# Reordering the first batch of a fused attention and feed-forward kernel: scores further ahead, casts and copies on other engines, loads in another order

## The chip, the cores and the metric

The kernel runs on one core of a Trainium2 chip. The metric is the device time of one execution in microseconds; lower is better. Executions of one kernel differ by 1 to 6 us here, so every comparison is made against executions of the kernel before on the same chip in the same rounds.

## The reference

Eight batches of eight heads of causal attention (576 positions, 64 wide, with a bias from a cumulative sum of `s`), then a gated feed-forward on all 4608 tokens:

```python
scores = q @ k.T / 8 ;  cum = cumsum(max(s, 0))
scores = where(causal, -1e9, scores + min(-(cum[i] - cum[j]), 0))
x = (softmax(scores) @ v)            # [B, H, 576, 64] -> [4608, 512]
g = x @ w_gate                       # 512 x 1536
out = (g * sigmoid(g) * (x @ w_val)) @ w_out
```

Inputs and output are float32; the kernel computes in bfloat16 with float32 sums.

## The kernel before

Heads are taken in half-batches of four. A half-batch's q and k are loaded ("raw"), cast to bfloat16 (ck, cq), transposed on TensorE and copied from PSUM into one of two KQ buffers; 64 more rows of KQ hold the bias, split into parts (HL), brought by small DMAs (`aug`). For each head TensorE makes scores, ScalarE takes the exponential, GpSimd masks the diagonal, TensorE multiplies with V (AV), VectorE normalises (ot), and TensorE transposes into x. The first batch of eight heads runs alone. After that the feed-forward of one tile of 512 tokens and the attention of the next batch are interleaved in one fixed TensorE order.

```python
# one queue (Sync) issues nearly all loads, in program order
def load_one(hb, name, rs=(0, NR)): ... nc.sync.dma_start(loaded[name, hb] ...)   # 2304-byte pieces
def load_v(b, cs):
    ...                                # one raw V buffer; rows of 64 floats: 256-byte pieces
    nc.sync.dma_start(t[0:n, c, :, :], v[b, :, c*128 : c*128+n, :].rearrange("h p d -> p h d"))
...
def prep_one(hb, i):                   # a quarter of a half-batch's q and k into KQ
    pe_transpose(hb, nm, g)
    pe_out(hb, nm, g, 0, nc.vector)
    pe_out(hb, nm, g, 1, nc.scalar)
...
def first_batch():
    avq = {4: (0,), 5: (1, 2), 6: (3, 4), 7: (5, 6, 7)}     # AV pieces behind head h's scores
    wq = {0: ("g", 0), 1: ("v", 0), 3: ("g", 1), 5: ("v", 1)}   # weight loads, GpSimd's queue
    for h in range(H):
        for ci in range(4):
            score_piece(h, ci)
        ...
    init_vt(1)
    aug(3, SP4)                        # Sync queue from here:
    load_v(1, range(5))                # V of batch 1
    load_qk(3)                         # k and q of half-batch 3
    load_qk(4)
    x_pe(H // 2 - 1)
...
hook = {                               # while the first feed-forward tile runs
    1: [cast_one(2, "k"), cast_one(2, "q")],
    2: [prep_one(2, 0)], 3: [prep_one(2, 1)], 4: [prep_one(2, 2)], 5: [prep_one(2, 3)],
    8: [cast_one(3, "k", nc.gpsimd), cast_one(3, "q", nc.gpsimd)],
    21: [load_qk(5)],
}
```

(Cuts are marked; the hook's lambdas are abbreviated.)

The softmax here doesn't subtract the row's maximum and nothing guards it: scores larger than these inputs give would overflow.

## Time and profile before

| | before |
|---|---|
| time, median of the first three runs | 409.08 us (407.78 to 409.84) |
| span of the profiled execution | 406.5 us |
| TensorE busy | 384.8 us, 95% |
| first feed-forward matmul | 34.40 us |
| first scores of the second batch | 46.51 us, after a wait of 2.52 us |

The prediction below shows the slices, the windows and the waits that it rests on. A line is start, length, engine, source line, operation, tiles and count; in brackets the idle time before it and what ended that.

```profile
44.90 1.15 POOL L230 CAST ck<-rawk 128x1152 bf16<-128x1152 f32 x1 [11.20 <-DMA rawk<-in_k_dram]
```
```profile
48.40 0.72 PE L272 MATMUL bank<-ident,ck 128*128 128x128 bf16 x5
```

GpSimd waited 11.20 us for k of half-batch 3 and cast it as soon as it landed, at 44.90. TensorE took up the result at 48.40, without a wait. So the transfer had 2.35 us to spare (48.40 - 44.90 - 1.15), in a kernel that the change wanted to bring forward by 5 us.

### The profile page before, as it was taken

The page shows a single profiled execution, that of the slowest core. Times are in us where ns is not written, and L with a number is a line of the kernel's source. Part 1 is how long each engine was busy: PE and PEld are TensorE (multiplying, and loading weights), DVE is VectorE, ACT ScalarE, POOL GpSimd, SP SyncE. Part 2 cuts the span into 40 slices and gives each one's busy share as a digit, 9 for nine tenths or more (in the row PEclk, how much of TensorE's full clock was granted, in tenths as well). Part 3 has the DMA queues.
Part 4 walks back from the last instruction along what each step waited for, and adds up shares of the span by engine and source line. Part 5 has one row for each costly group of instructions (what it writes and reads, how often), then busy time and mean ns, then how long its engine had stood idle before and what let it go on. Part 6 is the DMA issues. An engine that isn't in the chain of part 4 may idle for free.

```text
span 406.5 us, 8052 instructions
## 1 busy us (share of the span) xinstructions
PE 384.8 (95%) x3100; PEld 213.0 (52%) x3100; DVE 249.1 (61%) x487; ACT 212.0 (52%) x407; POOL 125.0 (31%) x225
## 2 busy tenths in 40 slices
PE   2778799999999999999999999999999999999996
PEld 2664355655555555555555555555555554444442
DVE  7755658547863696368835784489447733852760
ACT  6742566855555655555545654655555542322321
POOL 6852444732442235222613162316211110000000
PEclk9988899999999999999999999999999999999999
DMA  7999899398635784579356944681510002002002
GB/s 242 188 250 212 267 192 269 133 272 190 178 93 194 174 206 118 173 194 211 102 157 192 247 72 127 214 167 51 120 57 0 2 27 78 0 16 89 2 1 103
DMA packets 85288, 56.71 MB, mean 140 GB/s; under 512 B 65489, under 2 KB 69553, under 8 KB 85249
## 3 DMA queue, kind: packets, MB, share of 16 engines
q1 hardware_dynamic: 81440, 51.44, 47.0%
q0 software_dynamic: 3808, 4.76, 6.9%
q8 instruction: 24, 0.39, 0.4%
q14 instruction: 16, 0.12, 0.1%
HBM read 37.90 MB, written 15.93 MB: 132 GB/s over the span
## 4 chain that ended last, share of the span: by engine, by line
PE 89%; DVE 4%; ACT 2%; DMA 2%; POOL 1%; issue 1%; ACTq 0%; SPq 0%
PE bank L546 23%; PE bank L518 22%; PE bank L533 22%; PE bank L347 9%; PE bank L385 7%; PE bank L420 3%; PE wide L347 1%; DMA kq<-HL 1%; PE one L385 1%; DMA s_sb<-in_s_dram 1%; ACT th L523 1%; POOL vt L171 1%; DVE pp L525 1%; DVE kq L301 1%; ACT pt L360 1%
## 5 line engine op out<-in xcount | busy, mean ns | idle before, releaser
L360 ACT ACTIVATE pt<-bank 128x512 bf16<-128x512 f32 x224 | 104.2, 505 | 42.4 <-PE bank L347 35.1
L525 DVE SCALAR_TENSOR_TENSOR pp<-th,bank 128x512 bf16<-128x512 bf16 x108 | 74.2, 687 | 65.2 <-ACT th L523 64.6
L518 PE MATMUL bank<-xt,wg 128*128 128x512 bf16 x432 | 112.1, 382 | 0.7 <-DVE xt L425 0.7
L533 PE MATMUL bank<-xt,wv 128*128 128x512 bf16 x432 | 112.5, 383 | 0.0
L523 ACT ACTIVATE th<-bank 128x512 bf16<-128x512 f32 x108 | 64.5, 597 | 81.6 <-PE bank L518 79.8
L546 PE MATMUL bank<-wo,ht 128*128 128x512 bf16 x432 | 105.7, 379 | 0.0
L363 POOL TENSOR_SCALAR_AFFINE_SELECT pt<-pt 128x512 bf16<-128x512 bf16 x64 | 40.8, 638 | 127.1 <-ACT pt L360 124.7
L538 DVE TENSOR_TENSOR ht<-pp,bank 128x512 bf16<-128x512 bf16 x108 | 73.8, 684 | 7.4
L347 PE MATMUL bank<-kq 128*128 128x128 bf16 (+4 forms) x504 | 66.7, 241 | 3.3 <-DVE kq L301 2.5
L347 PEld LDWEIGHTS <-kq 128*128 128x128 bf16 x576 | 46.1, 100 | 40.2 <-issue 4.2
L518 PEld LDWEIGHTS <-wg 128*128 128x128 bf16 x432 | 38.6, 98 | 36.9 <-issue 1.9
L533 PEld LDWEIGHTS <-wv 128*128 128x128 bf16 x432 | 38.9, 99 | 35.2 <-issue 1.7
L546 PEld LDWEIGHTS <-ht 128*128 128x128 bf16 x432 | 38.1, 98 | 34.9
L385 PEld LDWEIGHTS <-pt 128*128 128x128 bf16 x960 | 41.1, 98 | 19.0 <-issue 1.9
L385 PE MATMUL bank<-vt,pt 128*128 128x65 bf16 x840 | 44.0, 194 | 0.0
L554 ACT ACTIVATE ysb<-bank 128x512 f32<-128x512 f32 x36 | 21.5, 597 | 42.9 <-PE bank L546 41.4
L368 POOL TENSOR_SCALAR_AFFINE_SELECT pt<-pt 128x64 bf16<-128x64 bf16 x64 | 15.3, 239 | 63.4 <-ACT pt L360 60.7
L402 DVE TENSOR_TENSOR ot<-bank,rc 128x320 bf16<-128x320 f32 x56 | 27.5, 492 | 1.9
L424 DVE COPY xt<-bank 128x128 bf16<-128x128 bf16 (+6 forms) x28 | 9.0, 321 | 31.7 <-PE bank L420 31.0
L401 DVE RECIPROCAL rc<-bank 128x5 f32<-128x5 f32 x56 | 10.6, 190 | 25.2 <-PE bank L385 25.2
L171 POOL CAST vt<-rawv 128x512 bf16<-128x512 f32 (+1 forms) x40 | 25.8, 673 | 0.0
L230 POOL CAST ck<-rawk 128x1152 bf16<-128x1152 f32 x15 | 17.4, 1159 | 11.5 <-DMA rawk<-in_k_dram 11.5
(59 smaller groups left out, 191.6 us busy)
## 6 DMA issues: line engine op xcount, KB each, us to landing
out_dram<-ysb SPq DMA_DIRECT2D x36, 256.0 KB
rawk<-in_k_dram SPq DMA_DIRECT2D x15, 576.0 KB
rawq<-in_q_dram SPq DMA_DIRECT2D x15, 576.0 KB
rawv<-in_v_dram SPq DMA_DIRECT2D x32, 256.0 KB
ks<-ck SPq DMA_DIRECT2D x11, 288.0 KB
qs<-cq SPq DMA_DIRECT2D x11, 288.0 KB
wg<-in_moe_w_gate_dram POOLq DMA_DIRECT2D x2, 768.0 KB, 12.0
wv<-in_moe_w_val_dram POOLq DMA_DIRECT2D x2, 768.0 KB, 13.6
```

The costliest lines, as they stand in the source:

```text
L171: eng.tensor_copy(VT[b % 2][0:n, c, :, 0:D], loaded["v", b][0:n, c, :, :])
L347: nc.tensor.matmul(sc[:, o : o + w], T[:, 1, e * S + 128 * tj : e * S + 128 * (tj + 1)], T[:, 0, e * S + lo : e * S + hi], start=True, sto ...
L360: nc.scalar.activation(pt[:, c0 : c0 + W], sc[:, 0:W], AF.Exp, scale=0.125)
L363: nc.gpsimd.affine_select(pt[:, 1088:1600], pt[:, 1088:1600], pattern=[[0, 4], [1, 128]], compare_op=ALU.is_ge, fill=zreg, base=0, channel ...
L385: nc.tensor.matmul(av[:, bi * (D + 1) : (bi + 1) * (D + 1)], pt[:, c0 : c0 + 128], VT[b % 2][:, tj, h, :], start=(tj == 0), stop=(tj == bi),)
L402: nc.vector.tensor_mul(ot[:, :, e * D : (e + 1) * D], av3[:, :, 0:D], rc[:, :, None].to_broadcast([128, NCH, D]),)
L518: nc.tensor.matmul(pg, WG[j][:, c, f0 : f0 + 128], xt[:, c, :], start=(c == 0), stop=(c == 3),)
L523: nc.scalar.activation(th, pg, AF.Tanh, scale=0.5)
L525: nc.vector.scalar_tensor_tensor(pp, in0=th, scalar=1.0, in1=pg, op0=ALU.add, op1=ALU.mult)
L533: nc.tensor.matmul(pv, WV[j][:, c, f0 : f0 + 128], xt[:, c, :], start=(c == 0), stop=(c == 3),)
L538: nc.vector.tensor_mul(ht, pp, pv)
L546: nc.tensor.matmul(py, hts[ft][:, ts_ * 128 : (ts_ + 1) * 128], WO[ft // WKO][:, ft % WKO, :], start=(ft == 0), stop=(ft == NFT - 1),)
```

## The change

Its intent: let the scores of the first batch run a head further ahead of AV, so that ScalarE's exponentials don't wait; split the V casts between GpSimd and VectorE; and copy half of half-batch 2's KQ on ScalarE before the feed-forward. To make the first scores earlier, q of half-batch 1 is loaded later. Two loads move with the code around them: V of batch 1 is now issued behind head 5, in front of the HL copies of half-batch 3, and the gate's second weight half moves by a head. The core of the diff (the zeroing of the bias rows and the size of a buffer of ones also change):

```diff
-        load_qk(1)
+        load_one(1, "k")
...
         cast_half(0, "k", 0, nc.scalar)
-        cast_half(0, "q", 0, nc.gpsimd)
+        cast_half(0, "q", 0, nc.scalar)
         aug(0, SP4)
+        load_one(1, "q")
         load_v(0, range(5))
         load_qk(2)
-        aug(1, [nc.gpsimd] * 4)
...
-        cast_one(1, "k", nc.gpsimd)
+        cast_one(1, "k", nc.vector)
...
-            avq = {4: (0,), 5: (1, 2), 6: (3, 4), 7: (5, 6, 7)}
-            wq = {0: ("g", 0), 1: ("v", 0), 3: ("g", 1), 5: ("v", 1)}
+            avq = {5: (0,), 6: (1, 2), 7: (3, 4, 5, 6)}
+            wq = {0: ("g", 0), 1: ("v", 0), 4: ("g", 1), 5: ("v", 1)}
...
+                    for c in range(3, 5):
+                        cast_v(0, c, nc.vector)
...
                 if h == 3:
-                    for c in range(3, 5):
-                        cast_v(0, c, nc.gpsimd)
                     aug(2, SP4)
+                    init_vt(1)
+                if h == 5:
+                    cast_one(2, "k", nc.gpsimd)
+                    load_v(1, range(5))
+                if h == 6:
+                    cast_one(2, "q", nc.gpsimd)
+                if h == 7:
+                    aug(3, SP4)
+                    load_qk(3)
+                    load_qk(4)
...
-            init_vt(1)
-            aug(3, SP4)
-            load_v(1, range(5))
-            load_qk(3)
-            load_qk(4)
+            for nm in ("k", "q"):
+                pe_transpose(2, nm, 0)
+                for r in range(2):
+                    pe_out(2, nm, 0, r, nc.scalar)
+            av_piece(7, range(NCH))
+            av_out(7)
             x_pe(H // 2 - 1)
...
-            1: [lambda: cast_one(2, "k", nc.gpsimd), lambda: cast_one(2, "q", nc.vector)],
-            2: [lambda: prep_one(2, 0)],
-            3: [lambda: prep_one(2, 1)],
-            4: [lambda: prep_one(2, 2)],
-            5: [lambda: prep_one(2, 3)],
-            8: [lambda: cast_one(3, "k", nc.gpsimd), lambda: cast_one(3, "q", nc.gpsimd)],
+            1: [lambda: prep_one(2, 2)],
+            2: [lambda: prep_one(2, 3)],
+            10: [lambda: cast_one(3, "k", nc.gpsimd), lambda: cast_one(3, "q", nc.gpsimd)],
```

The transposes of half-batch 3 also move by some steps in the fixed order of the second batch (the first from head 8 to head 9), and the second batch's attention starts after five items of the feed-forward instead of seven.

More of the change, by code (lines that the diff above doesn't have):

```diff
@@ L95 @@
     s_sb = const.tile([BH, S], FP32)
-    one_s = const.tile([BH, S], FP32)
+    one_s = const.tile([128, 1], FP32)
     c8 = const.tile([BH, S], FP32)
@@ L193 @@
             load_one(0, "q", (r, r + 1))
-        load_qk(1)
+        load_one(1, "k")
         nc.vector.memset(warm, 0.0)
+        nc.vector.memset(one_s, 1.0)
         nc.scalar.activation(warm, warm, AF.Exp)
-        nc.vector.memset(one_s, 1.0)
         nc.vector.memset(HL[:, 0:2, 0, :].bitcast(FP32), ONES2)
@@ L201, with pads @@
         make_identity(nc, ident)
+        def pads(i):
+            for r in range(2):
+                nc.gpsimd.memset(KQ[i][r][64 * r : 64 * r + 64, :, NR * S :], 0.0)
         for r in range(2):
-            nc.gpsimd.memset(aug_rows(0, r), 0.0)
+            nc.gpsimd.memset(aug_rows(0, r)[:, 1, :], 0.0)
             nc.scalar.mul(
-                KQ[1][r][64 * (1 - r) : 64 * (1 - r) + 64, 0, :],
-                one_s[:, 0:1].to_broadcast([64, NR * S + 64]), 0.0,
-            )
-        for r in range(2):
-            nc.gpsimd.memset(aug_rows(1, r)[:, 1, :], 0.0)
-            for i in range(2):
-                nc.gpsimd.memset(KQ[i][r][64 * r : 64 * r + 64, :, NR * S :], 0.0)
+                KQ[0][r][64 * (1 - r) : 64 * (1 - r) + 64, 0, :],
+                one_s[0:64, 0:1].to_broadcast([64, NR * S + 64]), 0.0,
+            )
+        pads(0)
         nc.vector.tensor_scalar(s_sb, s_sb, 0.0, 8.0, ALU.max, ALU.mult)
-        nc.vector.tensor_tensor_scan(c8, one_s, s_sb, 0.0, ALU.mult, ALU.add)
+        nc.vector.tensor_tensor_scan(
+            c8, one_s[0:BH, 0:1].to_broadcast([BH, S]), s_sb, 0.0, ALU.mult, ALU.add
+        )
         nc.vector.tensor_copy(HL[:, 0, 1, :], c8)
@@ L408, in av_out, with x_tiles @@
             pts.pop(bh)
+        def x_tiles(b, r):
+            for tt in ((0, 1) if b == 0 else (b + 1,)):
+                if r == 0:
+                    xts[tt] = xtp.tile([128, 4, TT], BF16, tag="xt", name="xt")
         def x_pe(pr):
@@ L412, in x_pe @@
             ot = ots.pop(pr)
-            for tt in ((0, 1) if b == 0 else (b + 1,)):
-                if r == 0:
-                    xts[tt] = xtp.tile([128, 4, TT], BF16, tag="xt", name="xt")
+            x_tiles(b, r)
             bs = take()
@@ L475, in prep_one @@
             pe_out(hb, nm, g, 1, nc.scalar)
-        PREP_AT = {(0, 3): 0, (1, 3): 1, (2, 1): 2, (2, 3): 3}
+        PREP_AT = {
+            2: {(1, 3): 0, (2, 1): 1, (2, 3): 2, (3, 1): 3},
+            3: {(0, 3): 0, (1, 3): 1, (2, 1): 2, (2, 3): 3},
+        }
         def attn_items():
@@ L492, in attn_items @@
                         yield kk + 0.1 + ci / 8
-                        if h + 1 < NPE and (step, ci) in PREP_AT:
-                            prep_one(h + 1, PREP_AT[step, ci])
+                        if (step, ci) in PREP_AT.get(h, ()):
+                            prep_one(h + 1, PREP_AT[h][step, ci])
                             yield kk + 0.1 + ci / 8
                 x = kk - 2
-                if x >= H and x % 2 == 1:
+                if H <= x < BH and x % 2 == 1:
                     x_pe(x // 2)
@@ L576 @@
         pe_out(0, "q", 0, 0, nc.vector)
-        pe_out(0, "q", 1, 0, nc.scalar)
+        pe_out(0, "q", 1, 0, nc.vector)
         cast_half(0, "k", 1, nc.scalar)
-        cast_half(0, "q", 1, nc.vector)
+        cast_half(0, "q", 1, nc.gpsimd)
+        for r in range(2):
+            nc.gpsimd.memset(aug_rows(1, r), 0.0)
+        aug(1, [nc.gpsimd] * 4)
+        pads(1)
         for nm, eng in (("k", nc.scalar), ("q", nc.vector)):
@@ L614, in first_batch @@
                         x_pe(p // 2 - 1)
-            init_vt(1)
-            aug(3, SP4)
-            load_v(1, range(5))
-            load_qk(3)
-            load_qk(4)
+            for nm in ("k", "q"):
+                pe_transpose(2, nm, 0)
+                for r in range(2):
+                    pe_out(2, nm, 0, r, nc.scalar)
+            av_piece(7, range(NCH))
+            av_out(7)
             x_pe(H // 2 - 1)
@@ L632, in pump @@
                     state["pos"] = 1e9
-        LAG = 1.65
+        LAGS = [0] + [1.65] * NTT
         hook = {
-            1: [lambda: cast_one(2, "k", nc.gpsimd), lambda: cast_one(2, "q", nc.vector)],
-            2: [lambda: prep_one(2, 0)],
-            3: [lambda: prep_one(2, 1)],
-            4: [lambda: prep_one(2, 2)],
-            5: [lambda: prep_one(2, 3)],
-            8: [lambda: cast_one(3, "k", nc.gpsimd), lambda: cast_one(3, "q", nc.gpsimd)],
+            1: [lambda: prep_one(2, 2)],
+            2: [lambda: prep_one(2, 3)],
+            10: [lambda: cast_one(3, "k", nc.gpsimd), lambda: cast_one(3, "q", nc.gpsimd)],
             21: [lambda: load_qk(5)],
@@ L644 @@
         for tt in range(NTT):
-            lo = H * (tt + 1) + (LAG if tt else 0)
-            hi = min(H * (tt + 2) + LAG, BH + 2)
+            lo = H * (tt + 1) + LAGS[tt]
+            hi = min(H * (tt + 2) + LAGS[tt + 1], BH + 2)
             span = 36
-            n0 = 7 if tt == 0 else 0
+            n0 = 5 if tt == 0 else 0
             n = 0
```

## The prediction

> **What bounds the kernel now.** I read the page's busy table and 40 slices first, then TensorE's work in windows, then the timeline of the first 66 us, and last the chain of waits there. The slices (PE is TensorE's busy share in tenths, PEclk its granted clock, one digit per 10.2 us):
>
> ```profile
> PE   2778799999999999999999999999999999999996
> PEclk9988899999999999999999999999999999999999
> DMA  7999899398635784579356944681510002002002
> ```
>
> From slice 7 to slice 39 TensorE is full. Only the first six slices can give time back, and the clock dips there, too. The windows (length; then busy time and count of PE, PEld, DVE, ACT, POOL; clock; DMA share; GB/s) cut where the clock changes:
>
> ```profile
> 23.80:27.20 3.40, 3.40 (x43) 2.65 (x39) 1.90 (x6) 1.55 (x3) 1.54 (x3) 0.51 1.13 258
> 27.20:34.00 6.80, 4.95 (x101) 3.95 (x99) 4.56 (x16) 2.84 (x4) 3.54 (x7) 1.00 1.16 213
> 34.00:37.50 3.50, 3.10 (x8) 1.17 (x9) 0.77 (x2) 0.60 (x1) 0.00 (x0) 0.51 1.16 214
> 37.50:43.98 6.48, 6.48 (x44) 3.26 (x41) 4.80 (x8) 2.30 (x4) 0.00 (x0) 1.00 0.98 241
> 43.98:46.51 2.53, 0.01 (x2) 0.01 (x1) 1.37 (x3) 1.13 (x3) 1.15 (x1) 1.00 1.04 390
> 46.51:47.80 1.29, 1.29 (x11) 0.84 (x12) 0.51 (x1) 1.27 (x3) 1.12 (x1) 0.98 1.05 405
> 47.80:51.20 3.40, 3.40 (x17) 1.89 (x16) 2.75 (x4) 2.10 (x6) 2.84 (x6) 0.51 0.30 92
> 51.20:66.00 14.80, 13.37 (x128) 7.82 (x127) 9.25 (x19) 10.38 (x21) 7.19 (x13) 1.00 1.15 193
> ```
>
> Three stretches of some 3.4 us run at half clock. Between 43.98 and 46.51 TensorE does nothing. The timeline (start, length, line, operation, count, idle time and what ended it) names two waits, and the chain of waits the third stretch:
>
> ```profile
> 22.28 0.31 PE L385 MATMUL one<-vt,pt 128*128 128x65 bf16 x5 [1.77 <-POOL vt L171]
> 34.40 1.86 PE L518 MATMUL bank<-xt,wg 128*128 128x512 bf16 x4 [0.70 <-DVE xt L425]
> 46.51 0.83 PE L347 MATMUL bank<-kq 128*128 128x128 bf16 x8 [2.52 <-DVE kq L301]
> ```
> ```profile
> 43.77 0.71 ACT kq L299
> 44.49 0.03 issue
> 44.51 0.61 ACT th L523
> 45.12 0.02 issue
> 45.14 0.69 DVE pp L525
> 45.83 0.63 DVE kq L301
> ```
>
> So the first feed-forward matmul starts at 34.40. At 46.51 the first scores of the second batch have waited 2.52 us for the copies that put half-batch 2's transposed q and k into KQ; these copies queue on VectorE and ScalarE between the feed-forward's own tanh and products. In the first batch ScalarE's exponentials set the pace (8 heads x (1.02 + 0.64) = 13.4 us), but they run from 13.0 to 31.3, 18.3 us: 5.1 us are three waits of 2.00, 1.85 and 1.28 us for scores that stand behind the attention-times-V matmuls (AV), the first of them behind the V casts.
>
> **What the Trainium skill says.** "TensorE: Matmul & The Clock Gate", Part 1, says that the clock halves after an idle window of about 3.4 us and comes back after a busy one. The trace agrees in size (3.4 us at 0.51 after the idle gap), but the clock also fell at 34.0 after 6.8 us with 4.95 busy, so a wholly idle window isn't needed here. The same page, Part 2, step 1: matmuls stay in program order and only weight loads are pulled ahead. The 1.77 us wait agrees: the next head's scores could not pass. "DMA: Bandwidth & Descriptors", Queues, rings and completion order: each DMA engine takes turns between queue rows; its section on issuing engines says transfers from different engines interleave. The trace has the DMA share at 1.1 to 1.2 from 14 to 34 us, so later bytes delay all the others. "SBUF — State Buffer", two separate sides: VectorE (in some modes) and GpSimd lock each other out of a shared port. This fits: the cast 128x1152 to bf16 took VectorE 1.14 us at 12.87 beside GpSimd and 0.75 at 37.59 with GpSimd idle.
>
> **The change part by part.** Four things move; the matmuls keep their number.
>
> *Start.* Rawq of half-batch 1 (0.59 MB) is issued behind the four small HL copies instead of ahead of them. In the trace these are issued from 8.26 and the last scores' operand lands at 11.88. With less in front I put them at 10.6 (8.26 + the 2.3 us that GpSimd's fastest HL copy took). But scores also stand behind the 18 transposes of the second half of q and k, which end at 11.76. ScalarE's k cast of that half moves from 8.92 to about 8.4 (one 0.71 copy goes to VectorE, one 0.66 cast comes, at 6.3 when q lands, and the copies follow it): transposes end near 11.2, first scores at 11.25 for 11.93. Gain 0.7 us, of scores only.
>
> *The price.* Rawq 1 is now issued at 11.1 rather than 3.99, beside V. At the 200 to 230 GB/s of these windows, 0.59 MB takes 2.6 us, plus some 2 us of latency: it lands near 15.3; the cast on VectorE (1.14) ends at 16.45. TensorE's transposes of it stand in front of heads 2 and 3; they end at 17.2 where before they ended at 15.86. So exponentials of head 2 start at about 17.8, not 16.50: the gain of the start is lost, and 0.6 more.
>
> *Scores a head further ahead.* From there the exponentials are to run nearly without a stop: 6 heads x 1.64 = 9.9 us, head 7 done at 27.7 instead of 31.3. V chunks 3 and 4 move to VectorE behind its eight KQ copies (5.64 us from 17.2, then two casts of 0.6): about 23.8, when AV 0 needs them at 23.2. A small wait.
>
> *GpSimd* takes on two casts (2.3 us) before head 7's mask and gives up the k cast and two V casts. Its queue from 8.6: cast 0.76, memsets 2.27, HL issues 2.50, pads 0.55, VT 0.81, mask and weight issues of heads 0 and 1 to 18.1, head 2 (waiting) to 19.7, V casts 21.5, head 3 and VT 23.2, head 4 and weights 24.9, head 5, weights and cast 27.6, head 6 and cast 29.7, head 7 30.5. TensorE arrives at the same place: scores of head 7 end near 26.5, then AV 3 to 6, three transposes of outputs and ten of half-batch 2, some 4.2 us with short waits, so AV 7 runs 30.7 to 31.3. Reciprocal, product (0.7), transposes (0.53), copies (0.53), starts: the feed-forward starts at about 33.4. **Gain 1.0 us**, and ten transposes (5 took 0.28 us of TensorE's time) no longer lie behind: **0.5**.
>
> *Half-batch 2.* Four of eight KQ copies are on ScalarE before the feed-forward (4 x 0.75 us in 30.3 to 33.5, where it was idle 5.02 us). Four stay, issued after the first gate and value groups, two on each engine. VectorE needs 0.69 + 0.70 + 0.68 + 0.70 us after the first tanh, so the last is done some 5.5 us after the start. The first scores come after three pairs of groups, 8 to 9 us after the start. The 2.52 us wait has no cause left: **gain 2.5**, and with it the half-clock stretch at 47.8, 3.4 x 0.49 = **1.7**. From 51.2 to 66 TensorE idles 1.43 us, part of it for copies of half-batch 3, which are now spread later: I take **0.5**.
>
> Sum 6.2 us. I take off 0.6 for waits that I can't see, so 5.6: 409.08 - 5.6 = 403.5.
>
> **Rivals.** (1) *The late rawq 1 and the shifted transfers decide.* All bytes after 12 us come 2.6 us later, and gate weights are issued 1.5 us later. The two weight loads landed within 13.6 us of issues at 14.9 and 16.6, so by 28.5 and 30.2; now perhaps 32.5 and 34.5, when they are needed at 33.4 and 35.3. If this or rawq is 1 to 2 us worse, the feed-forward starts at 34.4 to 35 and the time is about 405. For: the DMA share above 1. Against: rows are served in turn. (2) *GpSimd becomes the bound of the first batch.* Its queue ends at 30.5 by my count, level with TensorE; each 1.1 us cast in front of a mask moves AV. Blocked by VectorE's copies it gives 405 to 406. (3) *The half clock stays or moves.* If the clock at the feed-forward's start (3.5 us at 0.51 now) stays full because ten transposes fill the hole, 1.7 us more are won: 401.5. If a new idle stretch of 2 us (TensorE waiting for rawq 1 from 14.3 to 16.4) brings a half clock, it lies under ScalarE's exponentials and costs little. (4) *The start of the feed-forward is hidden by something later*: nothing speaks for it, since TensorE is full from 66 to 390.
>
> **Range and chances.** All of (1) and (2) against me: 407; all for me, with (3): 400.5. Two per cent faster is below 400.9, which needs nearly everything; the three runs of before spread by 2 us. So faster 0.15, within 0.83, slower 0.02.
>
> **What would show it.** Right: no idle of TensorE over 1 us between the feed-forward's start and 66; first scores near 11.3; exponentials of head 7 end near 28; feed-forward at 33 to 34; only one half-clock stretch after it, or none. Wrong: a wait on a DMA at the first gate or value group, a wait of AV on GpSimd's masks, a second half-clock stretch past 40 us, or the wait for KQ copies coming back at head 8.

## The result

The changed kernel took 413.9 us (median of four, 411.73 to 414.62) against 408.62 us for the kernel before (four runs). Ratios here and below are the mean time of one kernel's fast runs over that of the other's fast runs of the same rounds, so not quite the ratio of the medians: 1.0118, 95% interval 1.0069 to 1.0167. The change made the kernel 1.2% slower; the prediction was 403.5 us.

The slices of the page after (10.3 us each now):

```profile
PE   4777478999999999999999999999999999999996
PEclk9999979999999999999999999999999999999999
DMA  5999999186935693369245926690420002002002
```

The clock no longer dips in the third to fifth slice, as it did before, but in the sixth. TensorE's share falls to 4 tenths in the fifth slice (41 to 51 us), where it had 7 before, and to 7 in the sixth, where it had 9. The windows (length; busy time and count of PE, PEld, DVE, ACT, POOL; clock; DMA share; GB/s) cut around that hole:

```profile
34.40:46.50 12.10, 10.84 (x64) 5.58 (x66) 7.31 (x12) 7.72 (x15) 4.56 (x9) 1.00 1.09 188
46.50:54.07 7.57, 0.01 (x1) 0.00 (x1) 0.78 (x2) 0.47 (x2) 1.61 (x2) 0.78 1.10 322
54.07:57.50 3.43, 3.43 (x28) 2.33 (x29) 0.82 (x1) 1.33 (x2) 1.34 (x2) 0.50 1.15 284
```

TensorE stands still for 7.57 us while DMA works, and the other engines run out of work (busy for 0.47 to 1.61 us of it). The 3.43 us after it run at half clock. TensorE's timeline names the wait, and shows what the change achieved before it:

```profile
35.17 1.02 PE L528 MATMUL bank<-xt,wg 128*128 128x512 bf16 x3 [1.08 <-ACT kq L303]
...
40.79 0.82 PE L351 MATMUL bank<-kq 128*128 128x128 bf16 x8
...
54.07 0.71 PE L276 MATMUL bank<-ident,ck 128*128 128x128 bf16 x5 [7.57 <-POOL ck L234]
```

The first scores of the second batch (40.79) come without any wait, where before they came at 46.51 after 2.52 us. By 46.50 five gate groups, five value groups and 18 score matmuls are done. The kernel before has done the same 18 scores at 53.46, and one gate and one value group (0.86 us each) and five transposes (0.52 at half clock) more, so the equal point is at about 51.2: the changed kernel is 4.7 us ahead. Then it stops for k of half-batch 3. The chain of waits there:

```profile
45.50 7.25 DMA rawk<-in_k_dram
...
52.87 1.15 POOL ck L234
```

The load was issued at 45.50 only. The Sync queue's timeline, after and then before, says why:

```profile
23.05 19.36 SPq L164 DMA_DIRECT2D rawv<-in_v_dram  x5
42.52 2.89 SPq L185 DMA_DIRECT2D kq<-HL  x4
45.50 0.57 SPq L147 DMA_DIRECT2D rawk<-in_k_dram  x1
```
```profile
30.72 9.49 SPq L164 DMA_DIRECT2D rawv<-in_v_dram  x5
40.31 0.56 SPq L147 DMA_DIRECT2D rawk<-in_k_dram  x1
```

Five issues of V held the queue for 19.36 us instead of 9.49: they started 7.7 us earlier and ended 2.2 us later. The HL copies, which stand behind them now and stood in front of them before, took 2.89 us more. So the load came 5.2 us later, for a use that came earlier. Balance: 4.7 us won by 46.5, then 7.57 us of stop and 1.7 us of half clock (3.43 x 0.50) lost: 4.6 us slower, where the two spans differ by 5.1.

### The profile page after: what moved, and what is told of

Its sections match the earlier page's. It is cut to its first block, busy times and chain, and to the rows that moved or that the text cites. A ratio compares the mean times of both kernels' runs of the same rounds, so it can differ in the third digit from the quotient of the medians.

```text
span 411.6 us, 7995 instructions
## 1 busy us (share of the span) xinstructions
PE 382.4 (93%) x3046; PEld 214.1 (52%) x3100; DVE 247.8 (60%) x487; ACT 213.2 (52%) x409; POOL 123.9 (30%) x223
## 4 chain that ended last, share of the span: by engine, by line
PE 87%; DMA 4%; DVE 3%; ACT 3%; issue 2%; SPq 1%; POOL 0%; ACTq 0%; DVEq 0%; POOLq 0%
PE bank L556 22%; PE bank L528 22%; PE bank L543 21%; PE bank L351 9%; PE bank L389 7%; PE bank L427 3%; DMA rawq<-in_q_dram 2%; DMA rawk<-in_k_dram 2%; ACT pt L364 1%; PE wide L351 1%; ACT kq L303 1%; DVE pp L535 1%; DVE ht L548 1%; DVE ot L406 1%; PE one L276 0%
## 5 line engine op out<-in xcount | busy, mean ns | idle before, releaser
L528 PE MATMUL bank<-xt,wg 128*128 128x512 bf16 x415 | 110.7, 381 | 2.6 <-ACT kq L303 1.4
L543 PE MATMUL bank<-xt,wv 128*128 128x512 bf16 x412 | 109.4, 379 | 1.7 <-DVE xt L432 0.2
L556 PE MATMUL bank<-wo,ht 128*128 128x512 bf16 x415 | 103.6, 379 | 0.8
L351 PEld LDWEIGHTS <-kq 128*128 128x128 bf16 x576 | 47.2, 101 | 38.0 <-issue 4.8
L171 POOL CAST vt<-rawv 128x512 bf16<-128x512 f32 (+1 forms) x38 | 24.6, 674 | 0.0
L427 PEld LDWEIGHTS <-ot 128*128 128x128 bf16 (+1 forms) x160 | 12.2, 97 | 12.6 <-DVE ot L406 3.3
## 6 DMA issues: line engine op xcount, KB each, us to landing
wv<-in_moe_w_val_dram POOLq DMA_DIRECT2D x2, 768.0 KB, 15.3
```

The lines of the kernel that those rows point to most:

```text
L171: eng.tensor_copy(VT[b % 2][0:n, c, :, 0:D], loaded["v", b][0:n, c, :, :])
L351: nc.tensor.matmul(sc[:, o : o + w], T[:, 1, e * S + 128 * tj : e * S + 128 * (tj + 1)], T[:, 0, e * S + lo : e * S + hi], start=True, sto ...
L528: nc.tensor.matmul(pg, WG[j][:, c, f0 : f0 + 128], xt[:, c, :], start=(c == 0), stop=(c == 3),)
L543: nc.tensor.matmul(pv, WV[j][:, c, f0 : f0 + 128], xt[:, c, :], start=(c == 0), stop=(c == 3),)
L556: nc.tensor.matmul(py, hts[ft][:, ts_ * 128 : (ts_ + 1) * 128], WO[ft // WKO][:, ft % WKO, :], start=(ft == 0), stop=(ft == NFT - 1),)
```

## The experiments

Twelve kernels were run. Theory A says that only the order in the Sync queue is at fault. Theory B says that the transfers themselves are the limit of the first 50 us: whatever is put in front delays the rest, and bytes, small pieces and lost DMA time count. A third reading, that the new compute order gains nothing, is tested along the way. Times are medians; the ratio is to the kernel before in the same rounds.

| run | change to it | time us | ratio (95% interval) |
|---|---|---|---|
| changed kernel | | 413.9 | 1.0118 (1.0069 to 1.0167) |
| e1_qk3_first | k, q of half-batch 3 ahead of V | 415.01 | 1.0169 (1.0131 to 1.0208) |
| e2_v1_back | V back behind HL | 407.77 | 0.9976 (0.9934 to 1.0017) |
| e3_v1_early_alone | kernel before, V early | 408.59 | 1.0006 (0.9973 to 1.0038) |
| e4_q1_early | q of half-batch 1 back at the start | 412.22 | 1.0062 (0.9995 to 1.013) |
| e5_q1_and_v1_as_before | e2 and e4 together | 405.06 | 0.9913 (0.9869 to 0.9957) |
| e6_w_late | second weight halves later | 406.27 | 0.995 (0.9912 to 0.9988) |
| e7_v1_big_pieces | V in 2 KB pieces (wrong result) | 406.41 | 0.9959 (0.9917 to 1.0001) |
| e8_order_and_w_late | e5 and e6 together | 406.3 | 0.9928 (0.989 to 0.9966) |
| e9_gpsimd_relief | e5, GpSimd relieved at 40 to 46 us | 404.04 | 0.99 (0.9879 to 0.992) |
| e10_relief_and_copy | e9, one copy to VectorE | 408.69 | 1.0025 (0.999 to 1.006) |
| e11_av_as_before | e5, AV order of before | 405.63 | 0.9931 (0.9905 to 0.9956) |
| e12_prep_later | e9, transposes asked for later | 406.16 | 0.9944 (0.9902 to 0.9986) |

### The load that stopped TensorE, put first

```diff
                     cast_one(2, "k", nc.gpsimd)
+                    load_qk(3)
                     load_v(1, range(5))
...
                     aug(3, SP4)
-                    load_qk(3)
```

> The changed kernel with the loads of k and q of half-batch 3 put in the Sync queue ahead of the five V loads of batch 1 (all else the same). Theory A, order in the queue: the 7.57 us stop of TensorE at 46.5 us comes because these loads were issued at 45.5, behind V loads whose issue held the queue for 19.4 us and behind the HL copies; issued at about 23 they land before 35, the stop and the half clock behind it (1.7 us) are gone, and the time is about 413.9 - 9 = 405. Theory B, bytes: the DMA engines are full until about 50 us, so V of batch 1 now lands some 3 to 5 us later and the attention-times-V matmuls of head 8 wait for it instead; time 409 to 412.

It got slower: 415.01 us. The load is issued at 20.94 now, and yet TensorE waits 8.73 us for the same cast. The Sync queue and GpSimd's timeline of this run:

```profile
22.93 22.03 SPq L164 DMA_DIRECT2D rawv<-in_v_dram  x5
```
```profile
53.14 0.61 POOL L171 CAST vt<-rawv 64x512 bf16<-64x512 f32 x1 [5.11 <-DMA rawv<-in_v_dram]
...
54.49 1.13 POOL L234 CAST ck<-rawk 128x1152 bf16<-128x1152 f32 x1
```

V's issue takes 22.0 us, its last piece lands at 53.1, and the cast of k stands behind V's cast in GpSimd's queue. Theory A in its simple form falls: k's cast no longer waits for a transfer, and the wait has moved to V.

### The V loads alone, put back and put early

```diff
# e2, against the changed kernel
                     cast_one(2, "k", nc.gpsimd)
-                    load_v(1, range(5))
...
                     aug(3, SP4)
+                    load_v(1, range(5))
                     load_qk(3)
# e3, against the kernel before
+                if h == 5:
+                    load_v(1, range(5))
...
             aug(3, SP4)
-            load_v(1, range(5))
             load_qk(3)
```

> The changed kernel with only the five V loads of batch 1 put back to where the kernel before has them (behind the HL copies of half-batch 3, ahead of the loads of half-batch 3). Theory A: the HL copies are issued near 28 to 31, V from 31 to about 41, k of half-batch 3 at about 41 (before: 40.3); it lands near 45.5 and the stop shrinks from 7.6 to 1 us or less: time 405 to 407. Theory B: weights and V end at the same time as before, so the stop shrinks only by the 5.2 us by which the issue was late: time 407 to 409.

> The kernel before with only this part of the change: V of batch 1 is loaded behind head 5's scores, ahead of the HL copies of half-batch 3. Theory A: the V issue drags on until about 40, the HL copies and k of half-batch 3 are issued near 43 to 44, land near 49 to 50, and TensorE, which needs them at 48.4, waits 2 to 4 us: time 411 to 413. Theory B (nothing but bytes counts): same as before, 408 to 409.

Putting V back takes the time from 413.9 to 407.77, which lies in theory B's range; the stop of 1.65 us lies between what the two theories expected. V's issue still takes 13.55 us (28.39 to 41.94) and k is issued at 42.04, but its cast waits for no transfer: it follows V's casts in GpSimd's queue. In the kernel before, the early V costs nothing that can be seen (1.0006), as theory B had it. It does make k late there, too (issued at 44.23, waited for until 48.22), but TensorE takes it up at 49.86 only, because this kernel still waits 2.89 us for the KQ copies of half-batch 2 and started its feed-forward at 36.73 in this trace. So theory A's wait of 2 to 4 us was a miss. The early V hurts the changed kernel (e2) and not the kernel before, which still has the slack behind which the late k hides.

### q of half-batch 1 back at the start, then both

```diff
# e4, against the changed kernel; e5 has this and the edit of e2
-        load_one(1, "k")
+        load_qk(1)
...
         aug(0, SP4)
-        load_one(1, "q")
```

> The changed kernel with q of half-batch 1 loaded at the very start again, as in the kernel before. If the late load costs what I read from the trace (ScalarE idle 2.73 us ahead of head 2, then half clock, exponentials of head 7 end at 29.25), the feed-forward starts 1 to 2 us earlier than 35.17, but the stop on half-batch 3's k at 46.5 grows by nearly as much, because that wait is for a transfer: time 412 to 414. If instead the start of the feed-forward sets the end, 411.5 to 412.5.

> The changed kernel with both transfer moves undone (q of half-batch 1 at the very start, V of batch 1 behind the HL copies), so the Sync queue has the order of the kernel before. If transfers set the end (bytes in sequence), k of half-batch 3 is issued near 40 and lands near 45, the stop of TensorE at 46 is under 1 us, and the time is 404 to 406.5. If the gain of 5 us at 46 us that the trace of the changed kernel shows were an illusion of compute order, the time would stay at 408 or more.

Alone, q early gives 1.0062, not clear from 1. The time is as expected, but the stop that was to grow is smaller in the trace: it shows an execution of 406.83 us with a wait of 2.33 us for the cast of k, while the three other executions took 412.18 to 412.70; what happened in those no trace shows. Together with V it gives 0.9913, clearly faster than the kernel before. The four orders look like a sum: V's place is worth 1.4% (1.0118 to 0.9976), q's place 0.6% (1.0118 to 1.0062), both 2.05% (1.0118 to 0.9913). V's step is clear of the intervals; q's step is not. The traces show what q's place does to the transfers: in the first 12 us the DMA engines moved 167 GB/s in the changed kernel and 218 in e5. The missing 0.6 MB comes later, when DMA is full. The Sync queue and TensorE of e5:

```profile
26.80 12.80 SPq L164 DMA_DIRECT2D rawv<-in_v_dram  x5
39.69 0.56 SPq L147 DMA_DIRECT2D rawk<-in_k_dram  x1
```
```profile
33.30 1.02 PE L528 MATMUL bank<-xt,wg 128*128 128x512 bf16 x3 [1.08 <-ACT kq L303]
...
46.25 0.45 PE L276 MATMUL bank<-ident,ck 128*128 128x128 bf16 x5 [1.60 <-POOL ck L234]
```

k is issued at 39.69, 0.6 us earlier than in the kernel before. The stop is 1.60 us, more than the 1 us expected; the time of 405.06 us is in the expected range. The gain of the compute order is real and comes out once the transfers don't eat it. The clock of this trace has no half-clock dip in any slice of the page. The same lines of TensorE in e2, where only q is late:

```profile
34.89 1.02 PE L528 MATMUL bank<-xt,wg 128*128 128x512 bf16 x4 [1.07 <-ACT kq L303]
...
47.89 0.45 PE L276 MATMUL bank<-ident,ck 128*128 128x128 bf16 x5 [1.65 <-POOL ck L234]
```

e5 leads by 1.64 us at the end of the stop, and 1.59 us of that are there already at the feed-forward's start. In these two traces q's place acts on the first batch; that it holds up k's issue by 2.35 us (42.04 against 39.69) costs nothing up to there. Later it does: at 52.49 TensorE waits 0.67 us in e2 for the cast of q of half-batch 3, for which GpSimd had waited 3.46 us, and in e5 not at all.

### Why V's issue takes so long

```diff
# e6
-            wq = {0: ("g", 0), 1: ("v", 0), 4: ("g", 1), 5: ("v", 1)}
+            wq = {0: ("g", 0), 1: ("v", 0)}
...
+            w_load("g", 1)          # behind head 7
+            w_load("v", 1)
# e7: for batch 1 only, the same bytes from V read as contiguous rows
+                        t[0:n, c, :, :].rearrange("p h d -> p (h d)"),
+                        v[b].rearrange("h s d -> (h s) d")[c*1024 : c*1024 + 8*n, :].rearrange(...)
```

> The changed kernel with only the second halves of the gate and value weights (needed near 50 us) issued at the end of the first batch instead of behind heads 4 and 5. Theory: V's 256-byte pieces and the weights share the DMA engines from 24 to 40 us, which is what stretches the V issue to 19.4 us and holds k of half-batch 3 up. Then V issue takes under 12 us, k of half-batch 3 is issued before 38, the 7.57 us stop is gone or under 1 us, and the time is 404 to 407, unless the late weights stop the seventh gate group near 50 us. If V's issue is slow by itself, it stays near 19 us and the time near 413.

> The changed kernel with V of batch 1 read in 2048-byte pieces instead of 256-byte ones, the same number of bytes (gives a wrong result on purpose for batch 1: rows are taken in another order). If the size of the pieces makes the V issue long, it falls from 19.4 us to under 8, k of half-batch 3 is issued before 35 and the time is 403 to 406. If only bytes count, the issue stays above 14 us and the time at 411 to 414.

Both suspects are real, and both are theory B's. With the second weight halves out of the way, V's issue takes 9.53 us and the ratio is 0.995; the wait for the cast of k is 2.34 us instead of under 1, and again the cast follows V's casts on GpSimd without waiting for a transfer. With 2048-byte pieces instead of 256-byte ones (e7), the same bytes are issued in 5.17 us although the weights share the engines:

```profile
22.94 5.17 SPq L165 DMA_DIRECT2D rawv<-in_v_dram  x5
28.21 2.87 SPq L193 DMA_DIRECT2D kq<-HL  x4
31.30 0.39 SPq L147 DMA_DIRECT2D rawk<-in_k_dram  x1
```

So k is issued 14 us earlier than in the changed kernel, and the time falls to 406.41, a little above the expected 403 to 406. Its wait of 1.60 us for the cast stays and is therefore not the transfer. In both, q of half-batch 1 still comes late. So the old order and the late weights were tried together as well:

> Both remedies: the Sync order of the kernel before, and the second weight halves issued at the end of the first batch. Each transfer then comes roughly in the order in which it is needed: V near 30 to 36, k of half-batch 3 by 42. No stop over 1 us after the feed-forward's start, at most one half-clock stretch: time 402 to 404.5. If the late weights stop the seventh gate group, 405 to 408.

e8 (edits of e2, e4 and e6) gives 0.9928, no better than e5. Its issue of V still takes 11.09 us and the wait for the cast is 1.80 us. The expected 402 to 404.5 was missed.

### The 1.6 us that stay, and two more details

```diff
# e9, on e5
-            if bh == 8:                      # output weights
+            if bh == 10:
...
-            10: [lambda: cast_one(3, "k", nc.gpsimd), ...
+            10: [lambda: cast_one(3, "k", nc.vector), ...
# e10, on e9
-                    pe_out(2, nm, 0, r, nc.scalar)
+                    pe_out(2, nm, 0, r, nc.vector if (nm, r) == ("q", 1) else nc.scalar)
# e12, on e9
-            2: {(1, 3): 0, (2, 1): 1, (2, 3): 2, (3, 1): 3},
+            2: {(2, 1): 0, (2, 2): 1, (2, 3): 2, (3, 1): 3},
```

> The kernel of e5 with GpSimd relieved between 40 and 46 us, where it was busy without a break: the two loads of the output weights are issued two heads later and the k cast of half-batch 3 goes to VectorE. Theory: the 1.60 us that TensorE still waited for this cast in e5 came from GpSimd's queue (mask, weight issue, five V casts, mask, cast), not from the transfer; the wait falls below 0.7 us and the time to 0.3 per cent under e5: about 404. If the transfer of k sets it, the wait stays near 1.5 us and VectorE stalls with it: 405 to 406.

> e9 with the first transposes of half-batch 3 asked for some 2.4 us later in TensorE's order (behind head 10's second score piece instead of head 9's fourth), the last at the same place. e9 kept a wait of 1.60 us although the cast had changed its engine, so there its queue position, not the engine and not the transfer, held it. If TensorE simply asked too early, the wait falls below 0.4 us and the time to about 402.5 to 403.5. If closer transposes make the copies late for head 12, a wait for KQ copies comes near 62 us and the time stays at 404 or above.

What held the cast in e5, GpSimd's queue shows:

```profile
41.49 2.83 POOL L171 CAST vt<-rawv 128x512 bf16<-128x512 f32 x5
44.29 0.23 POOL L372 TENSOR_SCALAR_AFFINE_SELECT pt<-pt 128x64 bf16<-128x64 bf16 x1
44.48 0.62 POOL L367 TENSOR_SCALAR_AFFINE_SELECT pt<-pt 128x512 bf16<-128x512 bf16 x1
45.06 1.13 POOL L234 CAST ck<-rawk 128x1152 bf16<-128x1152 f32 x1
```

e9 has the lowest median, 404.04 us, as expected; its ratio of 0.99 has a narrow interval, which overlaps with those of e5 and e8, so it is not shown to be faster than they are. The reason is not the expected one: the wait is 1.60 us still, now for VectorE, which reaches the cast at 46.32 right behind its products of the feed-forward. e12 asks for the transposes later; the wait for the cast is gone from its trace, but waits of 0.39 and 0.15 us for KQ copies come up at 53.6 and 55.0, and the time is 406.16, with three executions near 405 and three above 407. Removing this wait gained nothing that the runs show, but the two traces don't compare cleanly: e12's feed-forward starts 0.76 us later than e9's (34.93 against 34.17). Putting the cast of k ahead of V's casts on GpSimd was not tried.

> e9 and one of the four copies of half-batch 2's KQ ahead of the feed-forward moved from ScalarE to VectorE. In e5 the first feed-forward matmul waited 1.08 us for ScalarE's last copy, 0.5 us after its own input was ready. Expected: that wait ends with the input's copy instead, the start comes 0.3 to 0.5 us earlier: about 403.6. If VectorE's extra copy delays the last output product, no gain.

e10's ratio lies 1.25 points above e9's, worse than either expectation. Its VectorE and TensorE:

```profile
33.01 0.83 DVE L305 COPY kq<-one 64x640 bf16<-64x640 bf16 x1 [2.23 <-ACT kq L303]
```
```profile
34.65 0.77 PE L427 MATMUL one<-ident,ot 128*128 128x128 bf16 x5 [3.30 <-DVE ot L406]
```

VectorE's copy waits 2.23 us for ScalarE's copies, and the normalisation of head 7 stands behind it in VectorE's queue. TensorE then waits 3.30 us, to save 1.08. A copy that looks free on an idle engine was put in front of the work that the start hangs on.

### Which part of the change carries the gain

```diff
# e11, on e5
-            avq = {5: (0,), 6: (1, 2), 7: (3, 4, 5, 6)}
+            avq = {4: (0,), 5: (1, 2), 6: (3, 4), 7: (5, 6)}
```

> The kernel of e5 with the order of scores and attention-times-V of the kernel before (scores no head further ahead), the rest kept. My prediction gave the scores part 1.0 us and the preparation of half-batch 2 the larger share (2.5 for the wait, 1.7 for the half clock). Expected: feed-forward starts 0.5 to 2 us later than in e5, no wait over 1 us for half-batch 2's copies, time 405.5 to 407. If the scores part carried the gain, the time is back at 408 to 409.

0.9931 against 0.9913 for e5, with overlapping intervals; the feed-forward starts at 33.68 instead of 33.30. Running the scores a head further ahead is worth little: no difference is shown. So most of the gain is in what remains in e11. The prediction's sum puts it down to half-batch 2's preparation by ScalarE; that part was not run alone, so this is by elimination.

## Why the prediction was wrong, point by point

- **First scores.** Predicted 11.25 us, measured 10.25. Right in direction.
- **The late q of half-batch 1.** Predicted to land at 15.3, measured 14.43 (VectorE's cast starts there). The size of the delay was right, and so was head 2 (exponentials predicted at 17.8, measured 17.73). What was missed is that the 0.6 MB also push later transfers back: in e4 k of half-batch 3 is issued at 42.89 instead of 45.50. How much of the loss that makes, the runs don't separate.
- **Exponentials.** Predicted to end at 27.7, measured 29.25. Score matmuls of a head took 1.4 to 1.5 us up to 20.2 us instead of 0.95, and head 7 waited 1.14 us behind AV.
- **GpSimd's queue.** Predicted to end at 30.5, measured 30.7. It was not the bound; rival 2 didn't happen.
- **Start of the feed-forward.** Predicted 33.4, measured 35.17: 1.5 us for the exponentials, and the first matmul waited for ScalarE's four copies, which ended at 35.12 and not at 33.5. A gain of 1.0 us was in truth a loss of 0.8.
- **Half-batch 2.** The 2.52 us wait is gone, and both half-clock stretches at 34.0 and at 47.8 with it. This step was right, and rival 3 (a full clock at the start) came out the good way.
- **The step that failed**: "I take off 0.6 for waits that I can't see". It measured 7.57 us of stop and 1.7 us of half clock. Rival 1 had the mechanism (the shifted transfers) but looked for it at the weights and at q of half-batch 1, and allowed 1 to 2 us. The transfer that decided was k of half-batch 3. It had 2.35 us to spare, and the line that says so was in the trace before: GpSimd waiting 11.20 us for it. I passed over that line because nothing on the chain waited for GpSimd. The prediction also gave V's issue no cost at all and never asked what would stand behind it.
- **Slips in its sums and readings.** 403.5 - 1.7 is 401.8, not 401.5; 11.1 + 2.6 + 2 is 15.7, not 15.3; 17.2 + 5.64 + 1.2 is 24.0, not 23.8. The DMA share from 14 to 34 us was 1.1 to 1.4 (1.34 and 1.37 up to 18 us). None of these decided.

With the two loads in their old places (e5), the kernel takes 405.06 us, 0.87% under the kernel before, some 3.6 us where 5.6 were predicted. That is inside the predicted range, by the predicted mechanism, but it is not the change that was predicted. Its feed-forward starts at 33.30, but the predicted 33.4 was for a late q, so that this agrees is partly luck.

## What to carry to other kernels

Before bringing compute forward, list for each load how long before its use it lands; the smallest of these slacks, not the compute sum, can cap the gain, and an engine off the chain that waits long for a DMA is where to find it. In a queue that issues in order, put loads in the order of their use, and don't put one of many small pieces in front of one that is needed sooner. When a load is moved later to help one early step, price both the step that waits for it and, while DMA is full, its bytes against everything behind it.

## What the Trainium skill lacked or had wrong

- "DMA: Bandwidth & Descriptors", Issuing engines are not separate DMA queues, says that the time to start a DMA is usually small relative to the DMA itself. Here five V issues held the Sync queue for 19.36 us (12.80 in e5, 9.53 in e6), and all loads behind them with it. What holds the issue back, no run shows.
- The same page, Why small descriptors are slow, gives the DMA engine's overhead for 256-byte pieces (27%). It gives no time for the issue, and neither does "Perfetto Trace Analysis", What "DMA-bound" means, which names a queue full of issues as a bound that larger descriptors relieve: 256-byte pieces took 19.36 us to issue beside the weights, 2048-byte pieces of the same bytes 5.17 us.
- "TensorE: Matmul & The Clock Gate", Part 1, gives an idle window as the cause of the half clock, and a later section of the part says that frequent short idles can do it, without a measure. Here the clock of the kernel before fell at 34.0 us after 6.80 us in which TensorE was busy for 4.95 (1.92 of the last 3.40).
- The same part warns that clock events in a trace can't always be trusted. A case with numbers: in the changed kernel the nine score matmuls of the first four heads took 1.51, 1.49, 1.54 and 1.41 us, up to 20.2 us, and 0.95 us in the next head, while the record reads 1.00 throughout. In the kernel before, nine of them took 1.52 us in a stretch recorded at 0.51.
